# Moving W2's last quarter, two PSUM tiles and the row sums in a fused attention and FFN kernel

## The chip, the cores and the metric

The kernel runs on one core of a Trainium2 chip. The metric is device time in microseconds (us) of that core. A profiled execution also leaves a trace. In it PE is TensorE (matmuls), DVE is VectorE, ACT is ScalarE, POOL is GpSimd. The trace's span is about 2 us shorter than the device time (248.8 against 250.83 us before the change).

## The reference

Eight batches, 8 heads, 576 rows, head dimension 64. Attention goes through 32 memory slots, then a residual feed-forward block follows (cut to what matters):

```python
a   = softmax(phi, axis=rows)                       # 576 x 32 per head
k_m = einsum('bhsm,bhsd->bhmd', a, k)               # 32 x 64
v_m = einsum('bhsm,bhsd->bhmd', a, v)
x   = softmax(q @ k_m.T / sqrt(64)) @ v_m           # 576 x 512 over all heads
xn  = (x - mean(x)) / sqrt(var(x) + 1e-6) * g_ln
out = x + relu(xn @ w_ch1) @ w_ch2                  # 512 -> 2048 -> 512
```

## The kernel before

W1 is multiplied with `v_m` of each batch ("fold", `a_w1b`), so that the first FFN product (`mm1`) works on the attention weights `Eh` directly. The mean over features is folded into W1 as well (`w1_mean`, `m_copy`, once per piece of W1). `mm2` is the product with W2, for tiles of 128 rows, in steps 0 to 16 over the hidden dimension (the 16 steps of `mm1` are called tiles in the prediction). Short names: `kv` are the products `k_m` and `v_m`, `hl` GpSimd's row sums as two bf16 parts, `sc` the scores of q, `den` the sums under the second softmax, `Eh` the finished attention weights, `x_sb` the rows of x, to which the output step adds. `mm1(1)` is `mm1` for batch 1. The program's order is each engine's order: in the trace of before TensorE stands 0.22 us for v at 42.95 us while W2 matmuls that need no v are next in the program. Waits are put in by tile: whoever touches a tile waits for whoever used it last.

PSUM (TensorE's output memory) is divided like this:

```python
def big(shape, dtype, name):      # up to 2 x 512 FP32 a partition, three of them
    return psum.tile(shape, dtype, name=name, tag="big", bufs=3)
def one(shape, dtype, name):      # up to 512 FP32 a partition, two of them
    return psum.tile(shape, dtype, name=name, tag="one", bufs=2)
```

The parts that the change touches (cut; `...` marks cuts):

```python
for n in range(4):
    w2_load(n)
phi1 = load_phi(1, nc.gpsimd); kv1 = load_kv(1); q1 = load_q(1)
...
def a_exp(b):                     # exp(phi); sums of it over the rows
    ...
    if b >= 2:                    # GpSimd adds the row blocks: 4 adds, a cast, a subtract -> hl
        ...
def a_sum(b, ps):
    if b < 2: kv_sum(b, ps)       # nine small matmuls on TensorE
    else: ...                     # two matmuls on hl
...
def a_qT(b, i):                   # transposes of q, half i
    split = b == 1 and i == 1
    if split: qs = [f([P, 1024], BF16, "qT_ps") for f in (big, one)]
    else:     q_ps = big([P, 2, 1024], BF16, "qT_ps"); ...
...
def mm2(pr, t, j0, j1, ps=None, finish=True):
    if j0 == 0:
        chs[(pr, t)] = one([P, C], FP32, "ch_ps") if ps is None else ps
    ...
def mm2_out(pr, t):               # out = ch * rstd + x on VectorE, then the store
    nc.vector.scalar_tensor_tensor(out=x, in0=ch_ps, scalar=rstd, in1=x, ...)
...
# batch 0 and batch 1 woven together
mm1(0, 2, 5);  w1_mean(3); m_copy(3); a_w1b(0, 2)
mm1(0, 5, 8);  w1_mean(4); m_copy(4); a_w1b(0, 3)
mm1(0, 8, 11); a_vb(0); mm1(0, 11, 16)
x_tiles(0, [0, 1]); x_tiles(0, [2, 3])
mm2(0, 0, 0, 4); mm2(0, 1, 0, 4); x_rstd(0, [0, 1]); x_rstd(0, [2, 3]); a_exp(1)
mm2(0, 0, 4, 16); mm2(0, 1, 4, 16); mm2(0, 2, 0, 8); a_kv(1); mm2(0, 2, 8, 12); a_tr(1)
a_qT(1, 0); a_w1b(1, 0); mm2(0, 2, 12, 16, finish=False); a_qT(1, 1); a_w1b(1, 1); a_sc(1)
mm2_out(0, 2); mm2(0, 3, 0, 4); a_w1b(1, 2); a_den(1); load(2); a_exp(2)
mm2(0, 3, 4, 12); a_w1b(1, 3); mm2(0, 3, 12, 16, finish=False); a_vb(1); mm2_out(0, 3)
# from here a loop: mm1(b), mm2, small products of batch b+1 between
```

The softmax here doesn't subtract the row's maximum and nothing guards it: scores larger than these inputs give would overflow.

Of the kernel before, what the change touches and what calls it, by code (L numbers as in the profile page):

```python
# [9 lines left out]
FP32 = mybir.dt.float32  # L10
# [6 lines left out]
def kernel(  # L17
# [17 lines left out]
    P = 128  # L35
# [20 lines left out]
    def big(shape, dtype, name):  # L56
        return psum.tile(shape, dtype, name=name, tag="big", bufs=3)
# [38 lines left out]
    def load(b):  # L96
        loaded[b] = (phis[b] if b > 2 else load_phi(b, nc.gpsimd), load_kv(b), load_q(b))
# [37 lines left out]
    W1C = [slice(0, 256), slice(256, 512)] + [slice(512 * n, 512 * (n + 1)) for n in range(1, NCH)]  # L135
    for fs in W1C:
        nc.gpsimd.dma_start(out=w1r[:, :, fs], in_=w1_v[:, :, fs])
    for n in range(4):
        w2_load(n)
    phi1 = load_phi(1, nc.gpsimd)  # L140
    kv1 = load_kv(1)
    q1 = load_q(1)
    loaded[1] = (phi1, kv1, q1)

    g_bf = consts.tile([P, 4], BF16, name="g_bf")
    gneg = consts.tile([P, 4, P], BF16, name="gneg")
# [37 lines left out]
    def a_exp(b):  # L184
        phi_st, kv, _ = loaded[b]
        e = att.tile([P, NS, 4, M], BF16, name="e_sb")
        nc.scalar.activation(out=e.rearrange("p c j m -> p j c m"),  # L187
                             in_=phi_st.rearrange("p j (c m) -> p j c m", m=M), func=AF.Exp)
        st8[b] = {"e": e, "kv": kv}
        if b >= 2:  # L190
            es = att.tile([P, P], FP32, name="es")
            ev = e.rearrange("p c j m -> p c (j m)")
            a4 = att.tile([P, 4, P], FP32, name="es4", bufs=1)
            nc.gpsimd.tensor_tensor(out=a4, in0=ev[:, 0:4], in1=ev[:, 4:8], op=ALU.add)  # L194
            a2 = att.tile([P, 2, P], FP32, name="es2", bufs=1)
            nc.gpsimd.tensor_tensor(out=a2, in0=a4[:, 0:2], in1=a4[:, 2:4], op=ALU.add)
            nc.gpsimd.tensor_tensor(out=es, in0=a2[:, 0], in1=a2[:, 1], op=ALU.add)
            nc.gpsimd.tensor_tensor(out=es, in0=es, in1=ev[:, 8], op=ALU.add)
            hl = att.tile([P, 2, P], BF16, name="hl")
            nc.gpsimd.tensor_copy(out=hl[:, 0], in_=es)  # L200
            nc.gpsimd.tensor_tensor(out=hl[:, 1], in0=es, in1=hl[:, 0], op=ALU.subtract)
            st8[b]["es"] = hl
# [40 lines left out]
        a_pool(b, ps)  # L243

    def a_sum(b, ps):
        if b < 2:
            kv_sum(b, ps)
        else:

            for i in range(2):  # L250
                nc.tensor.matmul(ps[:, 0, P:P + 2], st8[b]["es"][:, i, :], ones8,
                                 start=(i == 0), stop=(i == 1))
# [7 lines left out]
    def a_tr(b, k_part=True, v_part=True):  # L260
        s = st8[b]
        t_ps = big([P, 3, P], BF16, "kvT_ps")
        if k_part:
            kvT = att.tile([P, 3, P], BF16, name="kvT")
            s["kvT"] = kvT
            for g in range(2):
                nc.tensor.transpose(t_ps[:, g, :], s["k2"][:, g].rearrange("p a d -> p (a d)"), ident)
        kvT = s["kvT"]
        if v_part:
            nc.tensor.transpose(t_ps[:, 2, :], s["v2"].rearrange("p a d -> p (a d)"), ident)  # L270
        if k_part:
            nc.vector.tensor_copy(out=kvT[:, 0:2, :], in_=t_ps[:, 0:2, :])
        if v_part:
            nc.vector.tensor_tensor(out=kvT[:, 2, :].rearrange("p (j m) -> p j m", m=M),
                                    in0=t_ps[:, 2, :].rearrange("p (j m) -> p j m", m=M),
                                    in1=g_bf.unsqueeze(2).to_broadcast([P, 4, M]), op=ALU.mult)
            rsum = att.tile([P, 2], FP32, name="rsum")
            nc.vector.tensor_reduce(out=rsum, in_=s["v2"], axis=mybir.AxisListType.X, op=ALU.add)
            s["rsum"] = rsum
# [12 lines left out]
    def a_qT(b, i):  # L292
        q_bf = loaded[b][2]
        if i == 0:
            qTs[b] = att.tile([P, 4, NP, P], BF16, name="qT")
        if b > 1:

            nc.sync.dma_start_transpose(out=qTs[b].rearrange("p j n x -> p (j n) x"),
                                        in_=q_bf.rearrange("p j n x -> p (j n x)"))
            return  # L300
        split = b == 1 and i == 1
        if split:

            qs = [f([P, 1024], BF16, "qT_ps") for f in (big, one)]
        else:
            q_ps = big([P, 2, 1024], BF16, "qT_ps")
            qs = [q_ps[:, u, :] for u in range(2)]
        for u in range(2):
            for n in range(NP):
                nc.tensor.transpose(qs[u][:, P * n:P * (n + 1)], q_bf[:, 2 * i + u, n, :], ident)  # L310
        dst = qTs[b][:, 2 * i:2 * i + 2].rearrange("p a n x -> p a (n x)")
        if split:
            nc.scalar.activation(out=dst[:, 0], in_=qs[0][:, 0:NP * P], func=AF.Copy)  # L313
            nc.vector.tensor_copy(out=dst[:, 1], in_=qs[1][:, 0:NP * P])
        elif i == 0 or b == 1:
            nc.scalar.activation(out=dst, in_=q_ps[:, :, 0:NP * P], func=AF.Copy)
        else:
            nc.vector.tensor_copy(out=dst, in_=q_ps[:, :, 0:NP * P])
# [82 lines left out]
    def mm1(b, j0, j1):  # L401
        s = st8[b]
        if b % 2 == 0 and j0 == 0:
            pair[b // 2] = moe.tile([P, JC, 2 * S], BF16, name="rT", bufs=1)
        rT = pair[b // 2]
        off = S * (b % 2)
        for j in range(j0, j1):
            h_ps = big([P, 2, 512], FP32, "h_ps")
            for g in range(2):
                for half in range(2):  # L410
                    nc.tensor.matmul(  # L411
                        h_ps[:, half, 0:HS], s["w1b"][:, g, P * j:P * (j + 1)],
                        s["Eh"][:, g, HS * half:HS * (half + 1)],
                        start=(g == 0), stop=(g == 1))
            dst = rT[:, j, off:off + S].rearrange("p (a x) -> p a x", a=2)
            if j % 3 != 1 if b == 0 else j % 3 or j == 0:
                nc.scalar.activation(out=dst, in_=h_ps[:, :, 0:HS], func=AF.Relu)  # L417
            else:
                nc.vector.tensor_scalar(out=dst, in0=h_ps[:, :, 0:HS], scalar1=0.0, scalar2=None,  # L419
                                        op0=ALU.max)  # L420
# [43 lines left out]
    def x_rstd(pr, ts):  # L464
        _, mv, _, n = xs[(pr, ts[0])]
        rstd = moe.tile([P, 2], FP32, name="rstd", bufs=4)
        nc.scalar.activation(out=rstd[:, 0:n], in_=mv[:, 0:n, 1], func=AF.Ln, bias=eps_sb)  # L467
        nc.scalar.activation(out=rstd[:, 0:n], in_=rstd[:, 0:n], func=AF.Exp, scale=-0.5)
        for t in ts:
            x, _, i, _ = xs[(pr, t)]  # L470
            xs[(pr, t)] = (x, rstd[:, i:i + 1])
# [3 lines left out]
    def mm2(pr, t, j0, j1, ps=None, finish=True):  # L475
        rT = pair[pr]
        if j0 == 0:
            chs[(pr, t)] = one([P, C], FP32, "ch_ps") if ps is None else ps
        ch_ps = chs[(pr, t)]
        for j in range(j0, j1):  # L480
            nc.tensor.matmul(ch_ps, rT[:, j, P * t:P * (t + 1)], w2b[:, j, :],  # L481
                             start=(j == 0), stop=(j == JC - 1))
        if j1 == JC and finish:
            mm2_out(pr, t)
# [17 lines left out]
    def mm2_out(pr, t):  # L502
        ch_ps = chs[(pr, t)]
        x, rstd = xs[(pr, t)]
        nc.vector.scalar_tensor_tensor(out=x, in0=ch_ps, scalar=rstd, in1=x,  # L505
                                       op0=ALU.mult, op1=ALU.add)
        for u in range(2):
            lo = P * t + TS * u
            dst = out[2 * pr + lo // S].rearrange("(p c) x -> c p x", c=NS)
            nc.sync.dma_start(out=dst[CO[lo % S // TS]], in_=x[TS * u:TS * (u + 1), :])  # L510
# [36 lines left out]
    w1_mean(2)  # L547
    m_copy(2)
    a_w1b(0, 1)
    mm1(0, 2, 5)  # L550
    w1_mean(3)
    m_copy(3)
    a_w1b(0, 2)
    mm1(0, 5, 8)
    w1_mean(4)
    m_copy(4)
    a_w1b(0, 3)
    mm1(0, 8, 11)
    a_vb(0)
    mm1(0, 11, 16)  # L560

    x_tiles(0, [0, 1])
    x_tiles(0, [2, 3])
    mm2(0, 0, 0, 4)
    mm2(0, 1, 0, 4)
    x_rstd(0, [0, 1])
    x_rstd(0, [2, 3])
    a_exp(1)
    mm2(0, 0, 4, 16)
    mm2(0, 1, 4, 16)  # L570
    mm2(0, 2, 0, 8)
    a_kv(1)
    mm2(0, 2, 8, 12)
    a_tr(1)
    a_qT(1, 0)
    a_w1b(1, 0)
    mm2(0, 2, 12, 16, finish=False)
    a_qT(1, 1)
    a_w1b(1, 1)
    a_sc(1)  # L580
    mm2_out(0, 2)
    mm2(0, 3, 0, 4)
    a_w1b(1, 2)
    a_den(1)
    load(2)
    a_exp(2)
    mm2(0, 3, 4, 12)
    a_w1b(1, 3)
    mm2(0, 3, 12, 16, finish=False)
    a_vb(1)  # L590
    mm2_out(0, 3)
# [139 lines left out]
```

## Time and profile before

| | before |
|---|---|
| device time, median of 3 | 250.83 us (250.81 to 250.94) |
| span of the trace | 248.8 us |
| W2 products begin | 33.73 us |
| `den` of batch 1 begins | 50.12 us |
| `mm1(1)` begins, ends | 53.81, 62.24 us |

The first line below is the granted clock in 40 equal slices from the page (tenths, 9 means 90% or more). Lines from TensorE's timeline have start, duration, engine, line, operation, output<-inputs, shapes, count, and in brackets the idle time before it and who ended it.

```profile
PEclk9999999999999999999999999999999999999999
```

### The profile page before, as it was taken

What the parts mean: (1) busy time and instruction counts of PE and PEld (TensorE: products, weight loads), DVE (VectorE), ACT (ScalarE), POOL (GpSimd) and SP (SyncE); (2) the same over time, 40 slices, a digit from 0 to 9 for tenths busy, and PEclk for the clock granted to TensorE, in tenths of its full rate; (3) what the DMA queues carried; (4) which work ended last, traced back from release to release, by engine and by line L of the source; (5) the groups of instructions that cost most, each with busy time, mean ns of one, the idle gap of its engine ahead of it and who ended that gap; (6) DMA issues with size and microseconds to landing.
All of it is one profiled execution on the core that took longest, in us unless ns stands there. A gap on an engine that the chain in (4) does not pass through costs nothing.

```text
span 248.8 us, 5860 instructions
## 1 busy us (share of the span) xinstructions
PE 236.5 (95%) x2460; PEld 132.2 (53%) x2491; DVE 156.0 (63%) x304; ACT 130.0 (52%) x219; POOL 60.7 (24%) x100
## 2 busy tenths in 40 slices
PE   7979899999999999999999999999999999999994
PEld 2544554457544665467544674466544764476442
DVE  3247663685577656687569637685679538783641
ACT  3164572587554465837472656655580755465310
POOL 8643241022325402090206202170205001000000
PEclk9999999999999999999999999999999999999999
DMA  7999999998499799919965997429983301203133
GB/s 150 190 202 206 207 256 213 286 223 148 119 174 236 116 216 245 179 20 194 262 122 117 146 242 168 104 37 221 211 167 68 73 14 43 45 12 75 42 84 84
DMA packets 42451, 36.82 MB, mean 148 GB/s; under 512 B 17461, under 2 KB 37689, under 8 KB 42425
## 3 DMA queue, kind: packets, MB, share of 16 engines
q0 software_dynamic: 17776, 19.53, 46.9%
q1 hardware_dynamic: 24488, 16.79, 28.4%
q8 instruction: 19, 0.31, 0.5%
q10 hardware_dynamic: 160, 0.13, 0.2%
q14 instruction: 8, 0.06, 0.1%
HBM read 41.42 MB, written 9.44 MB: 204 GB/s over the span
## 4 chain that ended last, share of the span: by engine, by line
PE 77%; DMA 17%; issue 2%; ACT 2%; POOL 1%; DVE 0%; POOLq 0%
PE ch_ps L481 45%; PE h_ps L411 22%; DMA q_bf<-in_q_dram 8%; DMA w1r<-in_moe_w_ch_dram 6%; DMA kv_bf<-in_k_dram 3%; PE w1b_ps L390 3%; PE o_ps L442 2%; PE last_ps L493 1%; ACT x_sb L448 1%; PE sc_ps L328 1%; PE den_ps L359 1%; PE kv_ps L210 1%; POOL q_bf L92 1%; PE qT_ps L310 0%; ACT qT L313 0%
## 5 line engine op out<-in xcount | busy, mean ns | idle before, releaser
L481 PE MATMUL ch_ps<-w2b,rT 128*128 128x512 bf16 x531 | 123.0, 379 | 2.3 <-issue 1.6
L481 PEld LDWEIGHTS <-rT 128*128 128x128 bf16 x560 | 52.1, 98 | 63.5 <-issue 6.5
L411 PE MATMUL h_ps<-Eh,w1b 128*128 128x288 bf16 x512 | 66.4, 285 | 1.3 <-ACT rT L417 1.0
L417 ACT ACTIVATE rT<-h_ps 128x576 bf16<-128x576 f32 x88 | 52.2, 648 | 26.8 <-PE h_ps L411 26.8
L411 PEld LDWEIGHTS <-w1b 128*128 128x128 bf16 x512 | 49.5, 97 | 18.1 <-issue 2.4
L394 DVE SCALAR_TENSOR_TENSOR w1b<-m_sb,rsum,w1b_ps 128x512 bf16<-128x512 f32 (+1 forms) x66 | 44.2, 726 | 8.5 <-PE w1b_ps L390 6.1
L419 DVE TENSOR_SCALAR rT<-h_ps 128x576 bf16<-128x576 f32 x40 | 30.3, 758 | 25.2 <-PE h_ps L411 24.6
L505 DVE SCALAR_TENSOR_TENSOR x_sb<-ch_ps,rstd,x_sb 128x512 f32<-128x512 f32 x35 | 26.1, 745 | 9.5 <-PE ch_ps L481 6.4
L461 DVE BATCH_NORM_STATS2 bst<-x_sb 128x6 f32<-128x512 f32 x36 | 24.3, 676 | 6.4 <-ACT x_sb L448 6.4
L448 ACT ACTIVATE x_sb<-o_ps 128x1024 f32<-128x1024 f32 (+1 forms) x20 | 17.8, 939 | 16.1 <-PE o_ps L442 16.0
L287 POOL TENSOR_TENSOR vb<-v,vmask 128x256 bf16<-128x256 bf16 x12 | 7.8, 664 | 60.9 <-DVE rs L237 60.9
L194 POOL TENSOR_TENSOR es<-e_sb 128x512 f32<-128x512 bf16 x6 | 6.9, 1156 | 62.2 <-ACT e_sb L187 62.2
L467 ACT ACTIVATE rstd<-mv,eps_sb 128x2 f32<-128x2 f32 (+1 forms) x20 | 5.9, 297 | 30.8 <-DVE mv L462 30.6
L333 ACT ACTIVATE E_sb<-sc_ps,rs 128x640 bf16<-128x640 f32 x16 | 11.8, 790 | 12.8 <-PE sc_ps L328 12.8
L375 DVE SCALAR_TENSOR_TENSOR Eh<-E_sb,rs,rden 128x576 bf16<-128x576 bf16 x16 | 12.4, 814 | 8.8 <-ACT rden L374 8.8
L179 PE MATMUL w_ps<-fill 128*128 128x512 f32 (+1 forms) x16 | 10.5, 774 | 1.6 <-DVE fill L119 1.6
L227 DVE CAST k<-kv_ps 128x256 bf16<-128x256 f32 x7 | 3.0, 425 | 13.8 <-PE kv_ps L210 13.8
L390 PE MATMUL w1b_ps<-w1r,kvT 64*32 64x512 bf16 (+1 forms) x264 | 10.9, 374 | 0.1
L187 ACT ACTIVATE e_sb<-phi_st 128x1152 bf16<-128x1152 f32 x8 | 9.2, 1151 | 2.7 <-DMA phi_st<-in_phi_dram 2.7
L374 ACT ACTIVATE rden<-rden 128x576 f32<-128x576 f32 x16 | 10.0, 672 | 0.1
L92 POOL DMA_DIRECT2D q_bf<-in_q_dram x10 | 7.6, 757 | 4.6 <-DMA w2b<-in_moe_w_ch_dram 1.8
L210 PE MATMUL kv_ps<-kv_bf,e_sb 64*32 64x128 bf16 (+1 forms) x648 | 7.4, 215 | 0.7 <-DMA kv_bf<-in_v_dram 0.4
(76 smaller groups left out, 150.9 us busy)
## 6 DMA issues: line engine op xcount, KB each, us to landing
out_dram<-x_sb SPq DMA_DIRECT2D x70, 128.0 KB, 2.9
kv_bf<-in_k_dram POOLq DMA_DIRECT2D x7, 576.0 KB, 6.1
kv_bf<-in_v_dram POOLq DMA_DIRECT2D x7, 576.0 KB, 9.5
phi_st<-in_phi_dram SPq DMA_DIRECT2D x6, 576.0 KB, 4.9
q_bf<-in_q_dram POOLq DMA_DIRECT2D x6, 576.0 KB, 13.6
w2b<-in_moe_w_ch_dram POOLq DMA_DIRECT2D x4, 512.0 KB, 17.8
w1r<-in_moe_w_ch_dram POOLq DMA_DIRECT2D x3, 512.0 KB, 14.2
q_bf<-in_q_dram POOLq DMA_DIRECT2D x4, 288.0 KB, 12.6
```

The costliest lines, as they stand in the source:

```text
L179: nc.tensor.matmul(w_ps[:, 0:N], fill[:, 0:P], fill[:, 0:N], start=True, stop=True)
L333: nc.scalar.activation(out=E_[:, g].rearrange("p (a x) -> p a x", a=2), in_=sc[:, :, 0:HP], func=AF.Exp, scale=s["rs"][:, g:g + 1])
L375: nc.vector.scalar_tensor_tensor(out=Eh[:, g, :], in0=s["E"][:, g, 0:S], scalar=s["rs"][:, g:g + 1], in1=rd[:, g].rearrange("p a x -> p (a ...
L390: nc.tensor.matmul(ps[32 * j:32 * (j + 1), g, 0:N], s["kvT"][r:r + 64, 2, 32 * j:32 * (j + 1)], w1r[r:r + 64, j, fs], start=True, stop=Tru ...
L394: nc.vector.scalar_tensor_tensor(out=s["w1b"][:, g, fs], in0=m_sb[:, fs], scalar=s["rsum"][:, g:g + 1], in1=ps[:, g, 0:N], op0=ALU.mult, o ...
L411: nc.tensor.matmul(h_ps[:, half, 0:HS], s["w1b"][:, g, P * j:P * (j + 1)], s["Eh"][:, g, HS * half:HS * (half + 1)], start=(g == 0), stop= ...
L417: nc.scalar.activation(out=dst, in_=h_ps[:, :, 0:HS], func=AF.Relu)
L419: nc.vector.tensor_scalar(out=dst, in0=h_ps[:, :, 0:HS], scalar1=0.0, scalar2=None, op0=ALU.max)
L448: nc.scalar.activation(out=x[:, 0:n].rearrange("p i (u y) -> p i u y", u=2), in_=o_ps.rearrange("p u (i y) -> p i u y", i=2)[:, 0:n], func ...
L461: nc.vector.bn_stats(out=stt, in_=x)
L481: nc.tensor.matmul(ch_ps, rT[:, j, P * t:P * (t + 1)], w2b[:, j, :], start=(j == 0), stop=(j == JC - 1))
L505: nc.vector.scalar_tensor_tensor(out=x, in0=ch_ps, scalar=rstd, in1=x, op0=ALU.mult, op1=ALU.add)
```

## The change

Intent: bring batch 1's inputs in before the last quarter of W2, which is needed last; keep four output tiles open, so that TensorE has W2 work which doesn't need that quarter; do the means and folds of W1 one piece ahead in `mm1(0)`; take the row sums of batch 1 off TensorE.

```diff
--- before.py
+++ after.py
@@ -135,12 +135,13 @@
     W1C = [slice(0, 256), slice(256, 512)] + [slice(512 * n, 512 * (n + 1)) for n in range(1, NCH)]
     for fs in W1C:
         nc.gpsimd.dma_start(out=w1r[:, :, fs], in_=w1_v[:, :, fs])
-    for n in range(4):
+    for n in range(3):
         w2_load(n)
     phi1 = load_phi(1, nc.gpsimd)
     kv1 = load_kv(1)
     q1 = load_q(1)
     loaded[1] = (phi1, kv1, q1)
+    w2_load(3)
 
     g_bf = consts.tile([P, 4], BF16, name="g_bf")
     gneg = consts.tile([P, 4, P], BF16, name="gneg")
@@ -187,7 +188,7 @@
         nc.scalar.activation(out=e.rearrange("p c j m -> p j c m"),
                              in_=phi_st.rearrange("p j (c m) -> p j c m", m=M), func=AF.Exp)
         st8[b] = {"e": e, "kv": kv}
-        if b >= 2:
+        if b >= 1:
             es = att.tile([P, P], FP32, name="es")
             ev = e.rearrange("p c j m -> p c (j m)")
             a4 = att.tile([P, 4, P], FP32, name="es4", bufs=1)
@@ -243,7 +244,7 @@
         a_pool(b, ps)
 
     def a_sum(b, ps):
-        if b < 2:
+        if b < 1:
             kv_sum(b, ps)
         else:
 
@@ -298,13 +299,9 @@
             nc.sync.dma_start_transpose(out=qTs[b].rearrange("p j n x -> p (j n) x"),
                                         in_=q_bf.rearrange("p j n x -> p (j n x)"))
             return
-        split = b == 1 and i == 1
-        if split:
-
-            qs = [f([P, 1024], BF16, "qT_ps") for f in (big, one)]
-        else:
-            q_ps = big([P, 2, 1024], BF16, "qT_ps")
-            qs = [q_ps[:, u, :] for u in range(2)]
+        split = b == 1
+        q_ps = big([P, 2, 1024], BF16, "qT_ps")
+        qs = [q_ps[:, u, :] for u in range(2)]
         for u in range(2):
             for n in range(NP):
                 nc.tensor.transpose(qs[u][:, P * n:P * (n + 1)], q_bf[:, 2 * i + u, n, :], ident)
@@ -312,7 +309,7 @@
         if split:
             nc.scalar.activation(out=dst[:, 0], in_=qs[0][:, 0:NP * P], func=AF.Copy)
             nc.vector.tensor_copy(out=dst[:, 1], in_=qs[1][:, 0:NP * P])
-        elif i == 0 or b == 1:
+        elif i == 0:
             nc.scalar.activation(out=dst, in_=q_ps[:, :, 0:NP * P], func=AF.Copy)
         else:
             nc.vector.tensor_copy(out=dst, in_=q_ps[:, :, 0:NP * P])
@@ -413,7 +410,7 @@
                         s["Eh"][:, g, HS * half:HS * (half + 1)],
                         start=(g == 0), stop=(g == 1))
             dst = rT[:, j, off:off + S].rearrange("p (a x) -> p a x", a=2)
-            if j % 3 != 1 if b == 0 else j % 3 or j == 0:
+            if j not in (1, 6, 10, 12, 14) if b == 0 else j % 3 or j == 0:
                 nc.scalar.activation(out=dst, in_=h_ps[:, :, 0:HS], func=AF.Relu)
             else:
                 nc.vector.tensor_scalar(out=dst, in0=h_ps[:, :, 0:HS], scalar1=0.0, scalar2=None,
@@ -547,45 +544,49 @@
     w1_mean(2)
     m_copy(2)
     a_w1b(0, 1)
-    mm1(0, 2, 5)
+    mm1(0, 2, 4)
     w1_mean(3)
     m_copy(3)
     a_w1b(0, 2)
-    mm1(0, 5, 8)
+    mm1(0, 4, 8)
     w1_mean(4)
     m_copy(4)
     a_w1b(0, 3)
-    mm1(0, 8, 11)
+    mm1(0, 8, 12)
     a_vb(0)
-    mm1(0, 11, 16)
+    mm1(0, 12, 16)
 
     x_tiles(0, [0, 1])
     x_tiles(0, [2, 3])
-    mm2(0, 0, 0, 4)
-    mm2(0, 1, 0, 4)
+    c_ps = big([P, 2, 512], FP32, "ch2_ps")
+    cp = [None, None, c_ps[:, 0, :], c_ps[:, 1, :]]
+    for t in range(4):
+        mm2(0, t, 0, 4, cp[t])
     x_rstd(0, [0, 1])
     x_rstd(0, [2, 3])
+    load(2)
     a_exp(1)
-    mm2(0, 0, 4, 16)
-    mm2(0, 1, 4, 16)
-    mm2(0, 2, 0, 8)
+    for t in range(4):
+        mm2(0, t, 4, 8)
+    mm2(0, 0, 8, 12)
+    mm2(0, 1, 8, 12)
     a_kv(1)
     mm2(0, 2, 8, 12)
     a_tr(1)
+    mm2(0, 3, 8, 12)
     a_qT(1, 0)
     a_w1b(1, 0)
-    mm2(0, 2, 12, 16, finish=False)
     a_qT(1, 1)
     a_w1b(1, 1)
     a_sc(1)
+    mm2(0, 0, 12, 16)
+    a_den(1)
+    a_exp(2)
+    mm2(0, 1, 12, 16)
+    a_w1b(1, 2)
+    mm2(0, 2, 12, 16, finish=False)
+    a_w1b(1, 3)
     mm2_out(0, 2)
-    mm2(0, 3, 0, 4)
-    a_w1b(1, 2)
-    a_den(1)
-    load(2)
-    a_exp(2)
-    mm2(0, 3, 4, 12)
-    a_w1b(1, 3)
     mm2(0, 3, 12, 16, finish=False)
     a_vb(1)
     mm2_out(0, 3)
```

## The prediction

Its sum: 61.1 less 53.81 is +7.3, less 0.4 is +6.9; the balance of the waits gives +6.5; it takes 6.8 and comes to 257.6 us. With the cut paragraph goes its reason why no fourth big buffer could be had; that the new pair tile is one of the three stands in the diff (`c_ps = big(...)`). TensorE's wait for v at 42.95 us is 0.22 us; VectorE's copy of v began at 44.22 us, when ScalarE's of k (43.81, 0.38 us long) had ended. "The eighth transfer back" under C is read from the traces: in that of before GpSimd's issue of k at 20.78 us had waited 1.78 us, and the piece of W1 eight transfers back had landed at 20.50.

> **What bounds the kernel now.** I read the page first (busy shares, the 40 slices, the chain that ended last), then the chain in order of time, then the timeline of the first 56 us, because the diff touches nothing after batch 1's first product with W1 (`mm1(1)`). The page and the chain:
>
> ```profile
> PE 236.5 (95%) x2460; PEld 132.2 (53%) x2491; DVE 156.0 (63%) x304; ACT 130.0 (52%) x219; POOL 60.7 (24%) x100
> ...
> PE 77%; DMA 17%; issue 2%; ACT 2%; POOL 1%; DVE 0%; POOLq 0%
> ```
>
> TensorE is busy 95% of the span. From 55 us on the chain is TensorE line after TensorE line, so a delay before that point is not won back and a gain is kept: the time moves by what `mm1(1)` moves. The DMA 17% lies wholly before 45.2 us, in two pieces of the chain in order of time, which say that loads were in flight, not that TensorE stood still:
>
> ```profile
> 10.52 15.11 DMA w1r<-in_moe_w_ch_dram
> ...
> 25.91 19.24 DMA q_bf<-in_q_dram
> ```
>
> TensorE's own timeline shows how little it really stood still (start, duration, engine, line, operation, count, and in brackets the idle time before it and who ended it):
>
> ```profile
> 23.42 0.87 PE L411 MATMUL h_ps<-Eh,w1b 128*128 128x288 bf16 x4 [0.25 <-ACT rT L417]
> ...
> 26.83 0.65 PE L411 MATMUL h_ps<-Eh,w1b 128*128 128x288 bf16 x4 [0.25 <-ACT rT L417]
> ...
> 30.02 3.13 PE L411 MATMUL h_ps<-Eh,w1b 128*128 128x288 bf16 x24 [0.25 <-ACT rT L417]
> 33.08 0.71 PE L442 MATMUL o_ps<-vb,Eh 64*128 64x128 bf16 x16
> 33.73 8.81 PE L481 MATMUL ch_ps<-w2b,rT 128*128 128x512 bf16 x39
> ...
> 42.95 0.80 PE L210 MATMUL kv_ps<-kv_bf,e_sb 64*32 64x128 bf16 x72 [0.22 <-DMA kv_bf<-in_v_dram]
> ...
> 45.20 0.73 PE L310 MATMUL qT_ps<-ident,q_bf 128*128 128x128 bf16 x10 [0.30 <-DMA q_bf<-in_q_dram]
> ...
> 50.12 0.66 PE L346 MATMUL den_ps<-E_sb,blk 128*128 128x288 bf16 x4
> ...
> 53.65 1.21 PE L411 MATMUL h_ps<-Eh,w1b 128*128 128x288 bf16 x8
> ```
>
> From 33.73 to 53.81 us (where `mm1(1)` starts in the chain) are 20.08 us. The work in them: 64 W2 matmuls at 0.216 us (the chain has 8 in 1.73 us) are 13.8, batch 1's small products about 4.8, so only some 1.5 us are lost to late loads and copies. That is all the reordered middle can win. The three waits in `mm1(0)` are worth more than the 0.25 us printed: `mm1` runs at 7.96/16 = 0.50 us a tile (64 matmuls in 7.96 us later in the chain); 16 tiles, three 0.95 us means and three 0.34 us folds make 11.8 us, and 20.0 to 33.08 took 13.1.
>
> [...] at 42.95 us TensorE waits for v while W2 matmuls that need no v stand behind it. [...] VectorE's copy of v waited for ScalarE's of k out of the same buffer. [...] The trace has 1.16 us for the 512-element add (mixed types).
>
> **The change part by part.**
>
> *W1 pieces ahead.* Tile 4 moves behind the fold of piece 2, tile 11 ahead of the vb products; relus spread 11 on ScalarE, 5 on VectorE as before but at other tiles. Tile 4 no longer waits for its own fold (0.6 us). With the old durations I get: mean 3 at 23.04 (its W1 piece lands then), fold done 24.3, tile 6 waits 0.26 for the relu of tile 4, tile 7 0.15 for the fold's buffer, tile 10 0.3 behind the m_sb copy; tile 15 ends near 32.4, against 33.08. W2 starts about 33.05. Gain 0.65 us.
>
> *W2's last quarter behind batch 1.* Landings in the trace: W2 quarters at 28.1, 30.7, 33.2, 35.8; phi 37.4, k 40.0, v 42.9, q 45.2 and 47.1. One 512 KB piece is 2.6 us, so v lands near 40.3, q near 42.5 and 44.5, the quarter by 47. It is now first read after batch 1's scores, after 50: no wait. v's 0.22 and q's 0.30 us go.
>
> *Sums on GpSimd.* Nine small matmuls become two (0.3 us less). But they need the six GpSimd operations first, and these start only after the exp:
>
> ```profile
> 38.60 1.15 ACT L187 ACTIVATE e_sb<-phi_st 128x1152 bf16<-128x1152 f32 x1
> ```
>
> ```profile
> 54.04 1.16 POOL L194 TENSOR_TENSOR es<-e_sb 128x512 f32<-128x512 bf16 x1 [15.65 <-ACT e_sb L187]
> ...
> 57.70 0.43 POOL L201 TENSOR_TENSOR hl<-es,hl 128x128 bf16<-128x128 f32 x1
> ```
>
> 54.04 to 58.13 is 4.1 us for batch 2's chain. The exp stays behind both rstd pairs, so it shifts with x_sb and ends near 39.1; the sums are ready near 43.2. TensorE has again exactly 40 W2 matmuls before it: 33.05 + 8.65 = 41.7. It waits 1.5 us; kv ends about 44.1 (before: 43.75). The early v is worth nothing.
>
> *Four tiles open.* Batch 1's chain now rotates through two big buffers. The waits I read from the built program, with old durations: kvT and 8 W2 matmuls to 46.0; first q transposes to 46.65; the copy is now half ScalarE (0.70), then half VectorE (0.49), one after the other, as VectorE waits for ScalarE on the shared PSUM tile: 48.0. The second transposes wait for it (1.0 us), the second fold product for the first fold (0.75), the first scores for the second copy (0.2), the second scores for the first exp (1.0). Scores end near 51.6, tile 0 finishes 52.4, den starts 52.4 (before: 50.12).
>
> *The last wait, the largest.* The final four matmuls of tile 3 wait, in the built program, for VectorE's output step of tile 2: both halves are one PSUM tile. VectorE's queue up to there is: Eh twice, output of tile 1, the folds of pieces 2 and 3, output of tile 2. Before:
>
> ```profile
> 52.37 1.55 DVE L375 SCALAR_TENSOR_TENSOR Eh<-E_sb,rs,rden 128x576 bf16<-128x576 bf16 x2 [0.70 <-ACT rden L374]
> 53.83 1.40 DVE L394 SCALAR_TENSOR_TENSOR w1b<-m_sb,rsum,w1b_ps 128x512 bf16<-128x512 f32 x2
> 55.15 0.48 DVE L287 TENSOR_TENSOR vb<-v,vmask 128x256 bf16<-128x256 bf16 x2
> 55.55 0.74 DVE L505 SCALAR_TENSOR_TENSOR x_sb<-ch_ps,rstd,x_sb 128x512 f32<-128x512 f32 x1
> ```
>
> Eh starts 2.25 us after den (50.12 to 52.37): 54.65. From start to start: Eh pair 1.46, output 0.67, two fold pairs 1.32 each, then 0.75 for the output: 60.2. TensorE has issued everything else by 55.3, so it waits near 4.9 us, does four matmuls (0.86), and starts `mm1(1)` at 61.1.
>
> **Sum.** Before, `mm1(1)` began at 53.81; after, 61.1: +7.3 us. Before, it then lost some 0.4 us (16 tiles in 8.43 instead of 7.96) because Eh was just ready; now Eh is long done, so +6.9. In waits: 1.5 + 1.0 + 0.75 + 0.2 + 1.0 + 4.9 = 9.35 new, less old waits 1.5, less gain 0.65 and 0.3, less 0.4 in `mm1(1)`: about +6.5. The walk in time and the balance differ by 0.4 us of rounding; I take 6.8. 250.83 + 6.8 = 257.6.
>
> **The rivals.**
> *A. The intent holds:* earlier loads and larger reuse fill TensorE, the new waits hide. For it: the loads do end 19.24 us of the chain. Against it: TensorE lost only 1.5 us there. At best 1.5 + 0.65 + 0.3 + 0.4, about 248.
> *B. Two big buffers and the GpSimd wait hurt, but tile 3 doesn't wait* (VectorE gets to the output of tile 2 earlier, or that wait lies beside others): `mm1(1)` would then wait for Eh at about 55.4, +1.6 less 0.4: about 252. For it: VectorE is only 63% busy. Against: its queue is in order, and the folds, for which nobody waits, stand ahead.
> *C. GpSimd becomes the bound:* the sums come later still, behind `load(2)`, now ahead of them. Its last issue waits for k's landing (37.45, the eighth transfer back), so its queue should be free by 38.5, before the exp. If it waited for a later landing, 2 to 3 us more: about 260.
>
> **Range and chances.** The last wait is in the program; only its length is estimated. A gain in `mm1(0)` of 1.0 instead of 0.65, hidden hl and a shorter copy chain take 1.5 off; a slow GpSimd or DMA adds 1.5. Range 256.0 to 259.4. Slower by over 2% means above 255.85: 0.92. Within 2%: 0.06. Faster: 0.02.
>
> **What would show it.** On TensorE's timeline: a wait of 4 to 6 us for VectorE's x_sb before the last four W2 matmuls of batch 0, `mm1(1)` near 61; 1 to 2 us ended by GpSimd's hl before the kv sums; waits on the qT copy and the fold near 47 to 49; no wait for W2's last quarter. From `mm1(1)` on all is shifted alike. I am wrong if tile 3's matmuls start without that wait, or if `mm1(1)` starts before 59.

## More of the kernel before

The trace has a record of the clock that was granted to TensorE, where 1.00 is full speed.

```profile
48.00 0.87 PE L328 MATMUL sc_ps<-qT,kvT 64*32 64x320 bf16 x16
...
52.78 1.04 PE L481 MATMUL ch_ps<-w2b,rT 128*128 128x512 bf16 x4
```

The clock is full in every slice. Both scores products (`sc_ps`, 16 matmuls) run as one group without a bracket: with three big buffers nobody waits. Just before `mm1(1)` four W2 matmuls take 1.04 us, also without a wait.

## The result

The changed kernel took 260.71 us in the median of four runs (259.15 to 262.14; singly 260.04, 259.15, 262.14 and 261.38), the one before 250.82 us (250.74 to 250.94) in the same rounds. The ratio is 1.038 (95% interval 1.032 to 1.044): slower. The plain ratio of these means, or of the medians, is 1.039. The direction was as predicted; the median lies 1.3 us above the range of 256.0 to 259.4.

The traced execution is the one of 260.04 us. First its page: TensorE's busy time and the clock in 40 slices.

```profile
PE 239.3 (93%) x2453; PEld 133.6 (52%) x2484; DVE 156.6 (61%) x305; ACT 130.0 (50%) x219; POOL 63.9 (25%) x106
...
PEclk9999999978999999999999999999999999999998
```

TensorE does seven matmuls fewer than before and is nevertheless busy 2.8 us longer (239.3 against 236.5). Longer busy with less work means slower work, and the clock line has two slices under 9 where the line of before had none; the last slice is the end of the program.

TensorE's timeline where the prediction expected the waits:

```profile
42.61 0.18 PE L252 MATMUL kv_ps<-ones,hl 128*128 128x2 bf16 x1 [0.62 <-POOL hl L201]
...
47.90 0.72 PE L307 MATMUL qT_ps<-ident,q_bf 128*128 128x128 bf16 x10 [0.98 <-DVE qT L311]
49.21 0.41 PE L387 MATMUL w1b_ps<-w1r,kvT 64*32 64x512 bf16 x8 [0.60 <-DVE w1b L391]
...
51.18 0.33 PE L325 MATMUL sc_ps<-qT,kvT 64*32 64x320 bf16 x8 [0.91 <-ACT E_sb L330]
...
52.77 1.16 PE L343 MATMUL den_ps<-E_sb,blk 128*128 128x288 bf16 x4
...
60.84 1.02 PE L478 MATMUL ch_ps<-w2b,rT 128*128 128x512 bf16 x4 [3.68 <-DVE x_sb L502]
61.70 9.77 PE L408 MATMUL h_ps<-Eh,w1b 128*128 128x288 bf16 x64
```

All the predicted waits are there. The last four W2 matmuls wait 3.68 us for VectorE's output step. In VectorE's timeline one sees what stands before that step:

```profile
55.28 1.55 DVE L372 SCALAR_TENSOR_TENSOR Eh<-E_sb,rs,rden 128x576 bf16<-128x576 bf16 x2 [1.52 <-ACT rden L371]
56.75 0.75 DVE L502 SCALAR_TENSOR_TENSOR x_sb<-ch_ps,rstd,x_sb 128x512 f32<-128x512 f32 x1
57.41 2.71 DVE L391 SCALAR_TENSOR_TENSOR w1b<-m_sb,rsum,w1b_ps 128x512 bf16<-128x512 f32 x4
60.04 0.75 DVE L502 SCALAR_TENSOR_TENSOR x_sb<-ch_ps,rstd,x_sb 128x512 f32<-128x512 f32 x1
```

Eh twice, the output of tile 1, four fold operations, the output of tile 2: without a gap, as the prediction listed them.

Two rows have no counterpart in the prediction: `den` takes 1.16 us (0.66 before), and `mm1(1)` is slow. The chain in order of time (start, duration, what) shows this `mm1` against the next one:

```profile
61.87 9.60 PE h_ps L408 x64
...
92.97 7.96 PE h_ps L408 x64
```

The same 64 matmuls take 1.64 us more, without a wait. The windows view explains it. The columns are: window, its length, then busy time and count of instructions of PE, weight loads, DVE, ACT and POOL, then the granted clock, the DMA share and GB/s. The windows are laid at the edges of the clock's steps; each is 3.41 us long.

```profile
48.42:51.83 3.41, 1.59 (x29) 0.57 (x28) 2.55 (x5) 1.75 (x3) 0.00 (x0) 1.00 1.21 208
51.83:55.25 3.42, 3.33 (x10) 1.32 (x9) 0.75 (x1) 2.29 (x5) 0.00 (x0) 0.50 0.82 144
55.25:58.66 3.41, 1.91 (x21) 0.63 (x21) 3.38 (x5) 1.63 (x3) 1.63 (x2) 1.00 0.30 66
58.66:62.07 3.41, 1.23 (x8) 0.68 (x7) 2.70 (x7) 0.00 (x0) 1.85 (x5) 1.00 0.36 80
62.07:65.49 3.42, 3.42 (x17) 2.19 (x15) 0.66 (x2) 1.95 (x3) 0.00 (x0) 0.50 0.72 156
```

After a window in which TensorE worked 1.59 us of 3.41, and after one in which it worked 1.23, the whole next window ran at clock 0.50. Between the two drops lay two windows of full clock, 6.83 us. One long wait was not needed: the longest gap on TensorE in the 10 us before the first drop was 0.98 us.

So two theories stand for the miss. Theory: the waits are as predicted, and each is charged a second time, because a thinly used window makes TensorE half as fast in the next. Rival: the order itself, two buffers and late sums, costs more than the walk said, and the clock is incidental.

### The profile page after: what moved, and what is told of

It reads as the page before. It is cut to its first block, busy times and chain, and to the rows that moved or that the text cites. A ratio compares the mean times of both kernels' runs of the same rounds, so it can differ in the third digit from the quotient of the medians. Undisturbed runs are those within 1.5% of the kernel's fastest.

```text
span 258.3 us, 5858 instructions
## 1 busy us (share of the span) xinstructions
PE 239.3 (93%) x2453; PEld 133.6 (52%) x2484; DVE 156.6 (61%) x305; ACT 130.0 (50%) x219; POOL 63.9 (25%) x106
## 4 chain that ended last, share of the span: by engine, by line
PE 78%; DVE 6%; ACT 6%; DMA 3%; POOL 2%; issue 2%; DVEq 0%; POOLq 0%
PE ch_ps L478 41%; PE h_ps L408 25%; DMA kv_bf<-in_v_dram 3%; PE w1b_ps L387 3%; ACT x_sb L445 2%; PE o_ps L439 2%; DVE bst L458 1%; PE sc_ps L325 1%; PE last_ps L490 1%; DVE w1b L391 1%; PE kv_ps L211 1%; PE den_ps L356 1%; ACT rT L414 1%; DVE Eh L372 1%; ACT E_sb L330 1%
## 5 line engine op out<-in xcount | busy, mean ns | idle before, releaser
L478 PE MATMUL ch_ps<-w2b,rT 128*128 128x512 bf16 x531 | 124.3, 382 | 6.0 <-DVE x_sb L502 3.7
L414 ACT ACTIVATE rT<-h_ps 128x576 bf16<-128x576 f32 x88 | 52.5, 648 | 34.4 <-PE h_ps L408 34.4
L408 PE MATMUL h_ps<-Eh,w1b 128*128 128x288 bf16 x512 | 67.6, 290 | 0.9 <-ACT rT L414 0.5
L408 PEld LDWEIGHTS <-w1b 128*128 128x128 bf16 x512 | 50.4, 99 | 18.2 <-issue 2.4
L391 DVE SCALAR_TENSOR_TENSOR w1b<-m_sb,rsum,w1b_ps 128x512 bf16<-128x512 f32 (+1 forms) x66 | 44.1, 727 | 8.6 <-PE w1b_ps L387 5.7
L195 POOL TENSOR_TENSOR es<-e_sb 128x512 f32<-128x512 bf16 x7 | 8.1, 1154 | 61.3 <-ACT e_sb L188 61.3
```

The costliest lines, as they stand in the source:

```text
L391: nc.vector.scalar_tensor_tensor(out=s["w1b"][:, g, fs], in0=m_sb[:, fs], scalar=s["rsum"][:, g:g + 1], in1=ps[:, g, 0:N], op0=ALU.mult, o ...
L408: nc.tensor.matmul(h_ps[:, half, 0:HS], s["w1b"][:, g, P * j:P * (j + 1)], s["Eh"][:, g, HS * half:HS * (half + 1)], start=(g == 0), stop= ...
L414: nc.scalar.activation(out=dst, in_=h_ps[:, :, 0:HS], func=AF.Relu)
L478: nc.tensor.matmul(ch_ps, rT[:, j, P * t:P * (t + 1)], w2b[:, j, :], start=(j == 0), stop=(j == JC - 1))
```

## The experiments

Ten kernels ran, in three calls, each on another chip; all results were right. The kernel before was run beside each: its medians were 250.85, 250.90 and 250.75 us. The changed kernel was timed in rounds of its own, with before at 250.82 us, so differences between it and an experiment are between rounds.

### e1: fill the last wait with idle matmuls

```diff
     mm2_out(0, 2)
+    warm(4)          # four FP32 matmuls on constants
     mm2(0, 3, 12, 16, finish=False)
```

> The changed kernel with four idle FP32 matmuls put into TensorE's last wait (into a buffer that nobody reads). Theory: the half-clock stretch in the first product of batch 1 (62.07 to 65.49 us in the profile after) comes from TensorE standing idle in the 3.4 us before it. Then the wait for VectorE stays (the last four W2 matmuls still start near 60.8 us), but the 64 matmuls after it take 8.0 to 8.2 us instead of 9.6, no half-clock stretch starts after 58 us, and the time is 258.0 to 259.2. Rival: the clock falls for another reason (the chip, or the run): a half-clock stretch again in those matmuls in most runs, 260 to 262.

Measured: 258.67 us (257.93 to 259.35), ratio 1.031 (1.027 to 1.036). On TensorE's timeline:

```profile
61.38 1.02 PE L478 MATMUL ch_ps<-w2b,rT 128*128 128x512 bf16 x4 [0.73 <-DVE x_sb L502]
62.24 8.14 PE L408 MATMUL h_ps<-Eh,w1b 128*128 128x288 bf16 x64
```

More work, and yet 2.0 us less time than the changed kernel. `mm1(1)` takes 8.14 us instead of 9.77 in the same view, although it begins 0.54 us later. Only one half-clock window is left in this stretch, at 51.00 to 54.41. Two of the four runs had a mean clock of 1.00: 258.32 and 257.93 us. These are the runs that the prediction, made at full clock, described, and it said 257.6. The ranges of the two kernels just touch (259.35 and 259.15) and their rounds differ, so the trace is the better evidence. Its windows, over the wait and behind it:

```profile
57.83:61.24 3.41, 2.82 (x7) 1.05 (x6) 3.41 (x6) 0.00 (x0) 3.03 (x6) 1.00 0.35 77
61.24:64.65 3.41, 3.27 (x24) 2.29 (x24) 1.46 (x5) 1.72 (x3) 0.12 (x1) 1.00 0.43 96
```

TensorE is busy 2.82 us in the first, and the second has full clock. The theory holds for the second half-clock window of the changed kernel; the first one was not touched by this edit. (`mm1(1)` begins later here because the remaining half-clock window came 0.8 us earlier in this run and fell on more of the work ahead of VectorE's queue: `den` began at 53.31, not 52.77.)

### e2: the last four matmuls ahead of the output of tile 2

```diff
     a_w1b(1, 3)
-    mm2_out(0, 2)
     mm2(0, 3, 12, 16, finish=False)
+    mm2_out(0, 2)
     a_vb(1)
```

> The changed kernel with tile 3's last four W2 matmuls issued before VectorE's output of tile 2, so that they wait for nobody. Theory: that wait (3.68 us) goes, but the next thing in TensorE's queue needs a big buffer that VectorE's fold of piece 2 frees (about 58.8 us) and the third tile one freed by the fold of piece 3 (about 60.1), so the first product of batch 1 starts near 58.8 instead of 61.8 and stumbles once: 2.3 to 3 us less, and another 1.7 less if no half-clock stretch falls on it: 256 to 258.5. Rival: the wait was only hiding the same wait for VectorE's queue in full (everything up to the output of tile 2): less than 0.8 us gained, 260 or more.

Measured: 257.75 us (257.04 to 258.08), ratio 1.027 (1.023 to 1.032), 3.0 us under the changed kernel.

```profile
57.31 1.04 PE L478 MATMUL ch_ps<-w2b,rT 128*128 128x512 bf16 x4
59.49 0.66 PE L408 MATMUL h_ps<-Eh,w1b 128*128 128x288 bf16 x4 [1.14 <-DVE w1b L391]
```

The four matmuls no longer wait at all, although they write the same half of the pair tile as before. So their wait was for VectorE's reading of the other half of the pair tile, as the prediction had it. What came in its place: `mm1(1)` waits 1.14 us for a buffer that a fold still holds, and two waits for relus follow in it (0.74 and 0.25 us). Only one half-clock window is left here too, at 51.64 to 55.05. The 3.0 us are the shorter waits and the second window together.

### e3: the sums of batch 1 back on TensorE

```diff
-        if b >= 1:        # in a_exp
+        if b >= 2:
-        if b < 1:         # in a_sum
+        if b < 2:
```

> The changed kernel with the sums of batch 1 back on TensorE (nine small matmuls, as in the kernel before). Theory: TensorE waited for GpSimd from 41.8 to 43.1 us, and the whole chain behind it is a chain of latencies, so everything up to the first product of batch 1 comes 1.1 to 1.3 us earlier: 259.2 to 259.8 with the same clock losses. Rival: the wait is hidden, because a later one (q's landing, or W2's last quarter) takes it over: within 0.4 us of the changed kernel.

Measured: 259.11 us (258.16 to 260.86), ratio 1.034 (1.028 to 1.040), 1.6 us under the changed kernel. The kv products begin at 42.27 us instead of 43.22 and the last four W2 matmuls at 59.67 instead of 60.84. So the move to GpSimd, which was to save TensorE's nine small matmuls, costs about 1.2 us. The remaining 0.4 us is within the spread of the half-clock windows, as is the 0.1 us by which the median lies under the expected range.

### e4: only the W1 pieces and the relus, in the old order

```diff
-            if j % 3 != 1 if b == 0 else j % 3 or j == 0:
+            if j not in (1, 6, 10, 12, 14) if b == 0 else j % 3 or j == 0:
...
-    mm1(0, 2, 5)
+    mm1(0, 2, 4)       # and 4-8, 8-12, 12-16 after it
```

> The kernel before with only the reordered pieces of W1 and the moved relus. Theory: TensorE reaches the W2 matmuls 0.55 us earlier, as in the profile after, but then stands at the landings of v (42.9 us) and q (45.2 and 47.1 us), which are as late as before: 250.6 to 250.9, no gain. Rival: the gain of 0.55 us is kept, because the waits for v and q were a few tenths only: 250.2 to 250.4.

Measured, in 5 rounds: 250.78 us (250.17 to 251.01), ratio 1.000 (0.996 to 1.003): the same. In the traced run the first W1 piece landed later, and `mm1(0)` began at 20.39 us, 1.08 later than in the trace of before (19.31). From there to the first W2 product it took 13.95 us instead of 14.42: the pieces do gain 0.47. But the kernel waits for q all the same (0.23 us at 45.52), because q has not come earlier, and `mm1(1)` begins at 53.93. In the old order the loads of batch 1 decide, whether `mm1(0)` ends a little sooner or later.

### e5: the changed kernel with all of W2 early

```diff
-    for n in range(3):
+    for n in range(4):
         w2_load(n)
...
-    w2_load(3)
```

> The changed kernel with the last quarter of W2 loaded ahead of batch 1 again, as in the kernel before. Theory: in the changed order the earlier v and q buy nothing, because kv waits for GpSimd's sums until 43.2 us and the second q transposes wait for a copy until 47.9 us, both after the old landings (v 42.9, q 45.2 and 47.1 us): within 0.6 us of the changed kernel (260 to 261.3, by how many half-clock stretches a run catches). Rival: the loads are what the change lives on, and TensorE waits for v and q as before on top of the new waits: 262 or more.

Measured: 260.55 us (259.48 to 262.46), ratio 1.040 (1.035 to 1.044): as the changed kernel. The earlier loads are worth next to nothing in this order, because TensorE waits for GpSimd's sums and for the copies until about the time at which the later loads land: of all loads it waits here only for v, 0.18 us at 43.79. This run is also a check of the size of the last wait:

```profile
52.87 0.65 PE L342 MATMUL den_ps<-E_sb,blk 128*128 128x288 bf16 x4
...
60.67 1.86 PE L477 MATMUL ch_ps<-w2b,rT 128*128 128x512 bf16 x4 [4.63 <-DVE x_sb L501]
```

Here the clock's windows lay otherwise (the one before `den` from 49.42 to 52.83 us, with TensorE busy 1.78 us of it) and the first drop did not happen: `den` takes 0.65 us, and the wait is 4.63 us (predicted 4.9). The clock fell afterwards instead, at 59.66, for two windows, behind one in which TensorE did nothing.

### e6: a first repair

Sums on TensorE; q's first half transposed directly behind the kv products; the last W2 products of tile 3 ahead of the output of tile 2; the last two folds moved into `mm1(1)`. The diff is against the changed kernel, without the lines that only put the sums back and give q's second half to ScalarE whole.

```diff
     a_kv(1)
+    a_qT(1, 0)
     mm2(0, 2, 8, 12)
     a_tr(1)
-    mm2(0, 3, 8, 12)
-    a_qT(1, 0)
-    a_w1b(1, 0)
     a_qT(1, 1)
-    a_w1b(1, 1)
-    a_sc(1)
+    a_w1b(1, 0)
+    mm2(0, 3, 8, 12)
     mm2(0, 0, 12, 16)
-    a_den(1)
-    a_exp(2)
+    a_sc(1)
     mm2(0, 1, 12, 16)
-    a_w1b(1, 2)
+    a_den(1, finish=False)
     mm2(0, 2, 12, 16, finish=False)
-    a_w1b(1, 3)
-    mm2_out(0, 2)
     mm2(0, 3, 12, 16, finish=False)
-    a_vb(1)
+    mm2_out(0, 2)
+    a_den2(1)
+    a_w1b(1, 1)
+    a_exp(2)
     mm2_out(0, 3)
+    a_vb(1)
...
-    late = []
+    late = [lambda: a_w1b(1, 2), lambda: a_w1b(1, 3)]
```

> A repair of the changed kernel: late W2 quarter, pieces ahead and four open tiles kept; sums on TensorE; q transposed right after kv; scores and denominators ahead of most W2 matmuls of the last quarter, which fill the copies' latencies; outputs and folds ordered so that no matmul waits for VectorE's queue; the folds of pieces 2 and 3 inside the first product of batch 1. Theory (waits of the chain, then VectorE's queue, then the clock): the first product of batch 1 starts near 52.6 us, no half-clock stretch: 249.2 to 250.4, against 250.8 before. Rival (two big buffers alone are too few, whatever the order): 252 or more.

Measured: 255.85 us (255.44 to 256.30), ratio 1.020 (1.018 to 1.022), unclear at 2%, and 5.4 us above the upper end of what was expected. This expectation missed. The reason is on VectorE's timeline (first fence) and TensorE's (second):

```profile
53.17 2.43 DVE L372 SCALAR_TENSOR_TENSOR Eh<-E_sb,rs,rden 128x576 bf16<-128x576 bf16 x2
```

```profile
54.04 0.41 PE L408 MATMUL h_ps<-Eh,w1b 128*128 128x288 bf16 x2 [1.23 <-DVE Eh L372]
55.66 0.40 PE L408 MATMUL h_ps<-Eh,w1b 128*128 128x288 bf16 x2 [1.22 <-DVE Eh L372]
```

And on GpSimd's:

```profile
53.71 1.28 POOL L195 TENSOR_TENSOR es<-e_sb 128x512 f32<-128x512 bf16 x1 [15.19 <-ACT e_sb L188]
```

The two Eh operations take 2.43 us (1.55 in the changed kernel); the second alone takes 1.71 instead of 0.81. In just that time, from 53.71 us, GpSimd runs the first adds of batch 2's sums, and these take 1.28 and 1.12 us, where the changed kernel's adds took 1.15 and 0.72. The two gaps of 1.2 us left TensorE 0.81 us of work in a window, and the next one, from 56.42 to 59.83, ran at half clock. So the slow Eh (0.9 us longer) and the slow adds (0.13 and 0.40 us longer) ran at the same time. That they slow each other is the reading; no run here changes that alone. The rival of this expectation (two big buffers are too few in any order: 252 or more) is met by the time, and is not refuted.

### e7: the kernel before, with one big buffer held

```diff
     x_tiles(0, [2, 3])
+    held = big([P, 2, 512], FP32, "held_ps")
+    nc.tensor.matmul(held[:, 0, 0:64], ident, ident[:, 0:64], start=True, stop=True)
...
     mm2(0, 3, 12, 16, finish=False)
+    nc.tensor.matmul(held[:, 1, 0:64], ident, ident[:, 0:64], start=True, stop=True)
```

> The kernel before with one of the three big buffers held by two tiny matmuls from the x tiles to the end of batch 0, and nothing else changed. It prices the lost buffer alone, in the old order. Theory: the second scores wait for the first exp, the second denominators for the first log, so Eh is finished 1.3 to 2 us later: 252.0 to 253.0. Rival: the old order has enough W2 matmuls between the steps to hide it: under 251.3; or the lost buffer alone makes the whole loss: 256 or more.

Measured: 252.92 us (251.83 to 253.98), ratio 1.008 (1.003 to 1.012). The timeline of TensorE has waits that the kernel before has not:

```profile
50.62 0.33 PE L328 MATMUL sc_ps<-qT,kvT 64*32 64x320 bf16 x8 [0.88 <-ACT E_sb L333]
...
53.35 0.41 PE L346 MATMUL den_ps<-E_sb,blk 128*128 128x288 bf16 x2 [0.74 <-ACT rden L348]
```

The scores now come in two groups with a wait of 0.88 us between them, the same wait as the changed kernel's 0.91. So a long-held buffer costs some 2 us in the old order (252.92 against 250.90) by the loss of the third buffer alone; the two added matmuls take 0.19 us each at most. No half-clock window came here (mean clock 0.997, `den` 0.42 and 0.41 us for its two halves).

### e8: the kernel before, with only the late quarter of W2

```diff
-    for n in range(4):
+    for n in range(3):
...
     loaded[1] = (phi1, kv1, q1)
+    w2_load(3)
```

> The kernel before with only the load of W2's last quarter moved behind batch 1. Theory: tile 0 is finished before any other tile is opened, so TensorE stands from about 36.3 us until the quarter lands near 46 us; the rest of its work follows: the first product of batch 1 some 8 to 9 us later, with at least one half-clock stretch after the wait: 258 to 262. It shows why the four tiles had to be opened with it. Rival: something else fills TensorE, under 254.

One look, state unknown: 260.42 us. TensorE's timeline:

```profile
45.34 7.75 PE L482 MATMUL ch_ps<-w2b,rT 128*128 128x512 bf16 x24 [8.32 <-DMA w2b<-in_moe_w_ch_dram]
```

TensorE stood still for 8.32 us, and the clock was half from 40.02 to 50.26 us, three windows. So in this order the late load could not be had without opening more tiles, and opening more tiles is what took the buffer.

### e9: a second repair

As e6, but tiles 2 and 3 are finished first, with `den` between them; Eh stands ahead of the second fold and of outputs 0 and 1; `a_exp(2)`, which starts GpSimd's sums, comes after Eh.

```diff
     mm2(0, 3, 8, 12)
-    mm2(0, 0, 12, 16)
     a_sc(1)
-    mm2(0, 1, 12, 16)
-    a_den(1, finish=False)
     mm2(0, 2, 12, 16, finish=False)
-    mm2(0, 3, 12, 16, finish=False)
+    mm2(0, 3, 12, 14)
+    a_den(1, finish=False)
+    mm2(0, 3, 14, 16, finish=False)
     mm2_out(0, 2)
+    mm2_out(0, 3)
+    mm2(0, 0, 12, 16, finish=False)
     a_den2(1)
     a_w1b(1, 1)
+    mm2(0, 1, 12, 16, finish=False)
+    mm2_out(0, 0)
+    mm2_out(0, 1)
     a_exp(2)
-    mm2_out(0, 3)
```

> A second repair of the changed kernel, after the profile of the first (whose Eh waited in VectorE's queue behind the output of tile 2, whose second Eh took 1.71 us instead of 0.81 while GpSimd summed batch 2, and whose first tiles waited for buffers until 56.8 us). Now the pair tiles 2 and 3 are finished first, so that the long-held buffer comes free early; scores right after the q copies, denominators between the W2 matmuls; Eh ahead of the fold of piece 1 and of the outputs of tiles 0 and 1; the exp of batch 2, which starts GpSimd, after Eh. Theory (the loss is in the order of the queues, not in the two buffers as such): Eh finished near 52.5 us, first product of batch 1 under way by 52.5, no half-clock stretch in it: 249.6 to 251.0. Rival (two buffers are too few for this chain): Eh after 54 us and 252.5 or more.

Measured, in 5 rounds: 253.26 us (252.33 to 255.28), ratio 1.011 (1.007 to 1.015). It is 7.5 us better than the changed kernel, but still behind the one before, and above the 249.6 to 251.0 expected. The Eh pair is back at its usual time with GpSimd's sums moved out of its way:

```profile
53.67 1.54 DVE L372 SCALAR_TENSOR_TENSOR Eh<-E_sb,rs,rden 128x576 bf16<-128x576 bf16 x2
```

That agrees with the reading of e6, but e9 changes the order elsewhere too, so it does not isolate whether GpSimd's adds slow Eh. The clock stayed full from 22 us to past `mm1(1)`. Before that it was half from 18.37 to 21.78 us, and in this traced run (254.30 us) W2 began only at 35.34 us, so the end of Eh (55.21) can't be held against the expected 52.5 as it stands. Two runs with a mean clock of 1.00 took 252.33 and 253.11 us, so the early drop is not what misses the expectation. The rival of e9 (two buffers are too few) named 252.5 us or more, and the median meets it: whether another order would do with two buffers stays open. What stays are waits of 0.25 to 0.74 us for relus inside `mm1(1)`, where the moved folds and the relus of `mm1` take turns on the big buffers.

### e10: e4 with the stores of tiles 0 and 1 held back

The stores of the first two output tiles go out behind that of tile 2, so that they don't share the DMA engines with v and q of batch 1.

```diff
     def mm2_out(pr, t):
...
+        if (pr, t) in ((0, 0), (0, 1)):
+            held_out.append((pr, t, x))
+            return
+        for pr, t, x in [(pr, t, x)] + held_out:
             # the two stores
```

> The kernel before with the reordered pieces of W1, and the stores of tiles 0 and 1 held back until the store of tile 2 (about 50 us), so that they don't share the DMA engines with batch 1's q. In the kernel before, the first half of q took 2.24 us to follow v and the second 1.92, against 1.44 without stores. Theory: q lands near 44.4 and 45.8 us instead of 45.2 and 47.1, TensorE's wait for q goes, and the first product of batch 1 starts 0.3 to 0.8 us earlier: 250.0 to 250.5. Rival: v's landing (42.9 us, unmoved) sets the chain, so nothing is gained: 250.7 to 250.9.

Measured, in 5 rounds: 250.56 us (249.91 to 250.73), ratio 0.999 (0.996 to 1.002): the same. The effect on the loads is visible: from 30 to 50 us the stores' queue moved 0.52 MB in the kernel before and nothing here, and TensorE no longer waits for q. Its transposes of q begin at 44.77 and 46.73 us without a wait; in the kernel before they began at 45.20, after 0.30 us of waiting for q, and at 47.12, right behind the landing of q's second piece at 47.07. And `mm1(1)` begins 0.39 us earlier than in the trace of before (53.65):

```profile
53.26 1.21 PE L411 MATMUL h_ps<-Eh,w1b 128*128 128x288 bf16 x8
```

Before q it waits 0.63 us for v now, so part of the gain is taken back at once. The median lies between what the theory (250.0 to 250.5) and its rival (250.7 to 250.9) named. A gain of 0.2 to 0.4 us can't be told from the spread of the kernel before in these rounds (250.01 to 252.16). No version clearly beats the kernel before.

## Why the prediction was right or wrong

Right: that it is slower, and why. Point by point, in the order of the walk, predicted against measured in the traced run:

| step | predicted | measured |
|---|---|---|
| W2 products begin | 33.05 | 33.18 |
| GpSimd's sums ready; kv products end | 43.2; 44.1 | 43.05; 44.02 |
| waits for q's copy, fold, second copy, exp | 1.0, 0.75, 0.2, 1.0 | 0.98, 0.60, 0.31, 0.91 |
| `den` begins | 52.4 | 52.77 |
| Eh begins | 54.65 | 55.28 |
| output of tile 2 done | 60.2 | 60.79 |
| wait for it | 4.9 | 3.68 |
| `mm1(1)` begins | 61.1 | 61.87 |
| `mm1(1)` lasts | 7.96 | 9.60 |

**W1 pieces.** A gain of 0.65 was predicted and 0.55 came (33.73 to 33.18). e4 shows that alone, in the old order, it does not reach the time.

**The late quarter of W2.** It landed at 45.83 us and nobody waited for it, as predicted; e5 shows that the earlier v and q gain nothing that the times show.

**Sums on GpSimd.** Predicted to be the new wait ahead of the kv products. It is, at 42.61; undoing it in e3 moved kv 0.95 us ahead.

**Two big buffers.** The four waits came at nearly the predicted lengths, and e7 has two such waits in the old order, where the lost buffer alone costs 2 us.

**The last wait.** It is where the prediction put it, for the reason it gave (e2). VectorE's queue from Eh on took 5.51 us (55.28 to 60.79) against 5.55 predicted (54.65 to 60.2).

**The old waits.** The prediction let TensorE lose 1.5 us between 33.73 us and `mm1(1)` in the kernel before; the windows view of its trace has 0.83 (19.09 us busy of 19.92). Only the prediction's balance uses it, which would give +7.2 instead of +6.5; the walk in time does not.

**The step that failed** is the working of the sum, where the prediction goes from `mm1(1)` at 61.1 to "so +6.9": it set `mm1(1)` at the old 7.96 us, and every matmul before it at its old duration. Those are full-clock durations, and the clock had no term at all. Its term measured 2.4 us in the traced run. The first half-clock window, from 51.83, stretched `den` (0.66 to 1.16) and the W2 matmuls around it, and the 0.77 us by which `mm1(1)` began late is nearly all this: from the first kv product to the last four W2 matmuls it took 17.62 us here (43.22 to 60.84), and 16.88 (43.79 to 60.67) in e5, where this drop did not happen. The second, from 62.07, made `mm1(1)` 9.60 instead of 7.96: 1.64 us, about half of a 3.41 us window, as half speed would have it. 257.6 + 0.77 + 1.64 is 260.0, and the traced run took 260.04. The 3.68 us wait, shorter than predicted, is part of it: TensorE itself came to it at 57.16 (60.84 less 3.68) instead of 55.3, largely because it had worked slowly, while VectorE's queue was later by only 0.6. In e5, where the first drop did not happen, TensorE came at 56.04 and waited 4.63.

For the second window e1 shows that the idle wait was the cause and not a by-product: keeping TensorE at work in the wait, with nothing else changed, took 2.0 us off, and its two full-clock runs lie 0.3 and 0.7 us above the predicted 257.6. So the rival, that the order itself costs more than the walk said, has at most these 0.7 us.

**What could have been known.** A wait of 4.9 us can't be spread over windows of 3.41 us so that none is mostly idle: over two windows at least one gets 2.45 us of it, and over three the middle one is idle throughout. So, by what these runs showed, at least one half-clock window was to be expected, over work that is bound by TensorE, at a cost of up to 1.7 us. This takes the edge of about half a window that the runs gave (below), which the prediction did not have. With it the prediction would have been 259.3, and about 260 with a drop after the short waits as well.

**The rivals.** A (the intent holds) fell: nothing of the loads' gain reached `mm1(1)`. B (tile 3 doesn't wait) is nearly what e2 made by hand, and there it gave 257.75 and not 252, since the folds then hold the buffers that `mm1(1)` needs. C (GpSimd later still) did not occur: its adds began at 39.21, right behind the exp.

**Still open.** The spread of the changed kernel's four runs goes roughly with their mean clock (259.15 us at 0.993, 262.14 at 0.971), but the two between (260.04 at 0.984, 261.38 at 0.987) are in the wrong order, so the clock is not all of it. The kernel before isn't free of it either: one of its runs beside e1 took 253.29 us at a mean clock of 0.986, where most had 1.00 and 250 to 251. What TensorE still loses in e9 was seen as waits for relus but not undone by an experiment.

## What to carry to other kernels

When a change makes TensorE wait, charge the wait twice if it leaves TensorE busy for less than about half of a 3.41 us window, as here: once for its length, and once for the slower clock behind it, 1.64 us here for one such window at half clock, if TensorE is the bound there. Before opening a PSUM tile for long, count which chain rotates through the buffers that remain, and look at what stands in VectorE's queue ahead of the operation that gives the tile back. A kernel in which TensorE loses 0.8 us in the reordered stretch can't win more than that there, and an earlier load is worth nothing if the next wait behind it ends at the same time.

## What the runs show beyond the prediction

- The clock. Several short gaps were enough for a drop: in the changed kernel the longest in the 10 us before 51.83 was 0.98 us, but TensorE was busy only 1.59 us of the window of 3.41 before it. Laying windows at the edges of the clock's steps in the traces of eight kernels, between 14 and 72 us, ten windows of full clock came directly before a drop. TensorE was busy 0 to 1.64 us in nine of them (0.00 in e5, 0.41 in e8, 0.81 in e6, 1.23 and 1.59 in the changed kernel, 1.46 in e1, 1.59 in e2, 1.61 and 1.64 in e3), and 1.94 us in the tenth (small matmuls, in e9 before 18.37). Windows with 1.65 us (e2), 1.78 (e5) and 1.92 (the changed kernel) were not followed by a drop. So about half of a window was the edge here, but not a sharp one.
- Eh beside GpSimd's adds. In e6 they ran at the same time, and VectorE's second Eh operation took 1.71 us instead of 0.81, GpSimd's first two adds 1.28 and 1.12 us instead of 1.15 and 0.72. In e9 they ran one after the other for the most part, and the Eh pair took 1.54 us. No run separates this from the rest of the order.
- The pair tile. Two halves that software tracks as one tile made matmuls into one half wait for the reader of the other: 3.68 us, gone in e2 by the order alone.
